# Attention with a gated feed-forward on one core: block 0's x in two loads, clock-keeping products up to K's arrival, V's first half by ScalarE's queue, K's second half copied by two engines side by side

## The chip, the cores and the metric

The kernel runs on one core of a Trainium2 chip. The metric is the device time of one execution in microseconds (us), lower is better. Every time comes from a real execution; every profile is one execution taken by the hardware profiler. Times inside a profile count from the start of its span.

## The reference, cut to what matters

```python
# x (1, 2048, 640), k_cache and v_cache (1, 32, 2048, 192), all bf16
xn = layernorm(x)
q  = (xn @ wq)                      # 32 heads of 192
p  = softmax(q @ k.T * 192 ** -0.5) # per head
s  = (p @ v) @ wo
g  = silu(ffn(xn))                  # silu(xn @ w1) * (xn @ w3) @ w2
return x + s * g
```

Keys and values are given, so nearly all the work is 32 heads of scores, exponentials and values. The change concerns only the first microseconds, in which nothing can run before the first x and K have arrived.

## The kernel before: the parts that matter

The 2048 queries are four blocks of 512, and a head's keys are eight pairs of 128. The opening works on head 0 and block 0. Loads are issued by SyncE (`nc.sync`), ScalarE (`nc.scalar`) and GpSimd (`nc.gpsimd`), each in program order.

```python
pk1 = ps_o.tile([P, 4, 512], BF16, tag="ob1", name="pk1")
warm = pk1[:, 0, 0:2 * P].bitcast(F32)

def turn_over(k):                    # products that only keep TensorE busy
    for i in range(k):
        nc.tensor.matmul(warm, lhsT=ident_bf[:], rhs=ident_bf[:], start=True, stop=True)

def head_start():
    for t in range(4):
        load_x(0, t, t + 1, nc.scalar if t % 2 else nc.sync)
    load_k0(0, nc.sync)              # head 0's K, first half
    turn_over(24)
    ln_stats(0, 0); ln_stats(0, 1); ln_stats_act(0, 3)
    load_w0(nc.scalar)               # head 0's weights
    load_k0(1, nc.scalar)            # K, second half
    load_x(1, queue=nc.scalar)       # block 1's x, 640 KB
    ...
    load_v(0, (0,), nc.gpsimd)       # head 0's V, first half
    load_w(1)                        # head 1's weights, GpSimd
    for i in range(4): ln_norm(0, i, nc.vector)
    turn_k0(pk0, 0, range(4))        # 16 transposes of K
    turn_over(12)
    ln_turn(0, 0, nc.scalar.copy)    # 10 transposes of x, one copy to xnT
    turn_over(4)
    ln_turn(0, 1, nc.vector.tensor_copy)
    swap_halves(0)                   # xnS: xnT with its partition halves swapped, by DMA
    copy_k0(nc.scalar.copy, pk0, 0, 0); copy_k0(nc.scalar.copy, pk0, 0, 1)
    load_v(0, (1,))                  # V, second half, SyncE
    load_x(2)                        # block 2's x, SyncE
    project_first()                  # block 0's queries
    turn_k0(pk1, 1, range(4))
    copy_k0(nc.scalar.copy, pk1, 1, 0)
    copy_k0(nc.vector.tensor_copy, pk1, 1, 1)
    scores(0); shift_first()
    shift_k0()                       # VectorE: a part of K to other partitions
    scores(1)
    ln_stats(1, 0); ln_stats(1, 1); ...   # block 1's layer norm, VectorE

# the stream that follows; n counts pairs
    if h == 0 and qb == 0 and p == 3:
        project(1, 0)                # head 1's queries: needs xnS and head 1's weights
    scores(n + 2)
    values(n)                        # needs V
    # p == 2: ln_stats(2, 0) on VectorE, needs block 2's x
    # p == 3: ln_turn(1, 1): transposes of block 1's second pair, needs a PSUM buffer
    #         that VectorE's cast of head 1's queries gives back
```

V's tile has rows of 194 elements, of which the load writes 192 (the next holds ones), so that each of its 1024 pieces per half is 384 B long:

```python
queue.dma_start(out=vt[:, t * NPAIR:(t + 1) * NPAIR, 0:DH],
                in_=A_v_cache[0, h, t * HK:(t + 1) * HK, :].rearrange("(i s) d -> i s d", i=P))
```

## Time and profile before

| what | before |
|---|---|
| time | 1943.08 us, median of 3 (1942.95 to 1943.15) |
| TensorE (PE) busy | 1930.2 of 1941.6 us |
| TensorE busy in 20 to 40 us | 18.77 of 20.00 |
| first values (needs V) | 17.48 us |
| block 2's x awaited until | 24.10 us |
| transposes of block 1's second pair | 25.84 us |

First the page of the kernel before: busy time of each engine.

```profile
span 1941.6 us, 59662 instructions
...
PE 1930.2 (99%) x27269; PEld 1318.6 (68%) x27277; DVE 654.5 (34%) x997; ACT 1181.1 (61%) x1278; POOL 281.0 (14%) x499
```

Then the busy time by stretches of the kernel before: microseconds busy in each stretch for each engine, the granted clock of TensorE (1.00 is full), the busy share of the DMA engines, and GB/s.

```profile
16.00:20.00 4.00, 3.46 (x50) 2.23 (x51) 3.80 (x13) 3.15 (x4) 0.57 (x1) 1.00 1.19 195
20.00:24.00 4.00, 3.79 (x47) 2.08 (x43) 2.98 (x10) 1.33 (x3) 0.83 (x2) 1.00 1.09 218
24.00:28.00 4.00, 3.15 (x52) 2.31 (x49) 3.04 (x7) 1.90 (x3) 1.61 (x3) 1.00 1.25 241
```

The DMA engines are busy throughout. TensorE is idle here and there, and from 60 to 1460 us never. The timeline of the kernel before shows why. Columns: start, length, engine, line, operation, what it writes and reads, shapes, count; in brackets how long the engine was idle before, and what ended that.

```profile
6.09 1.89 PE L271 MATMUL pk<-ident_bf,kn 128*128 128x128 bf16 x16 [1.98 <-DMA kn<-in_A_k_cache_dram]
...
8.96 0.72 PE L354 MATMUL pst<-ident_bf,xn 128*128 128x128 bf16 x10
...
10.99 2.34 PE L391 MATMUL ps<-xnT,W 128*128 128x256 bf16 x20 [0.53 <-ACT xnT L356]
...
14.27 1.01 ACT L277 COPY KW<-pk 128x1024 bf16<-128x1024 bf16 x1 [0.52 <-PE pk L271]
...
15.31 0.69 DVE L277 COPY KW<-pk 128x1024 bf16<-128x1024 bf16 x1 [1.19 <-ACT KW L277]
...
16.56 0.42 DVE L281 COPY KW<-KW 64x1024 bf16<-64x1024 bf16 x1
...
17.48 0.83 PE L516 MATMUL obank<-vt,pT 64*128 64x193 bf16 x16
...
24.10 0.89 DVE L316 BATCH_NORM_STATS2 stats<-x_all 128x6 f32<-128x320 bf16 x2 [0.22 <-DMA x_all<-in_A_x_dram]
...
25.15 0.64 DVE L429 CAST qA<-ps 128x512 bf16<-128x512 f32 x1
...
25.84 0.73 PE L354 MATMUL pst<-ident_bf,xn 128*128 128x128 bf16 x10 [0.85 <-DVE qA L429]
```

VectorE (DVE) copies its part of K's second half only after ScalarE (ACT) is done with the other. From 15.31 it has work up to the query cast at 25.15, for which TensorE waits. It stops for any length only twice on the way: 0.81 us for a result of GpSimd (ahead of 23.08), and 0.22 us for block 2's x, the only load in this stretch that it waits for.

V's first half was issued at 8.33 us and had landed at 14.8, 2.7 us before it was needed.

### The profile page before, as it was taken

How to read it: one execution, taken by the hardware profiler on the slowest of the kernel's cores; microseconds unless marked ns; L12 is line 12 of the kernel's file. 1: busy time of each engine (PE TensorE's matmuls, PEld its weight loads, DVE VectorE, ACT ScalarE, POOL GpSimd, SP SyncE). 2: the span in 40 equal slices, each digit the busy share in tenths (PEclk: the TensorE clock that was granted, in tenths of full speed). 3: DMA queues.
4: the chain of work that ended last, by engine and by line, in shares of the span. 5: the costliest groups of instructions: out<-in, count | busy, mean ns of one | idle time of the engine just before them, and what ended most of it. 6: DMA issues, size and time to landing. Idle time of an engine off the chain costs nothing.

```text
span 1941.6 us, 59662 instructions
## 1 busy us (share of the span) xinstructions
PE 1930.2 (99%) x27269; PEld 1318.6 (68%) x27277; DVE 654.5 (34%) x997; ACT 1181.1 (61%) x1278; POOL 281.0 (14%) x499
## 2 busy tenths in 40 slices
PE   8999999999999999999999999999999999999998
PEld 5666666666666666666666666666666666577776
DVE  7433333333333333333333333333333334521111
ACT  5667776767776767776777777677767677210000
POOL 2111111111111111111111111111111110000000
PEclk9999999999999999999999999999999999999999
DMA  8643433323233434363434343334334220937883
GB/s 174 135 98 67 98 71 71 88 58 91 59 93 68 94 64 101 68 161 68 100 66 101 68 100 68 98 67 100 69 61 94 62 74 2 252 74 136 154 151 62
DMA packets 395747, 178.98 MB, mean 92 GB/s; under 512 B 342480, under 2 KB 384176, under 8 KB 395488
## 3 DMA queue, kind: packets, MB, share of 16 engines
q1 hardware_dynamic: 371072, 124.99, 31.1%
q0 software_dynamic: 19424, 45.78, 9.9%
q8 instruction: 215, 3.52, 0.8%
q10 hardware_dynamic: 4992, 4.33, 0.7%
q14 instruction: 44, 0.36, 0.1%
HBM read 52.82 MB, written 27.79 MB: 42 GB/s over the span
## 4 chain that ended last, share of the span: by engine, by line
PE 98%; DMA 1%; DVE 0%; ACT 0%; SPq 0%; issue 0%; DVEq 0%; ACTq 0%
PE obank L516 35%; PE st L487 33%; PE ps L424 14%; PE ps_s L111 11%; PE ps_f L728 3%; PE ps_gu L702 1%; PE st L488 1%; DMA x_all<-in_A_x_dram 1%; PE ps L410 0%; DMA kn<-in_A_k_cache_dram 0%; PE pk L271 0%; DVE stats L316 0%; PE pst L354 0%; SPq L289 0%; ACT xnT L356 0%
## 5 line engine op out<-in xcount | busy, mean ns | idle before, releaser
L490 ACT ACTIVATE pT<-st 128x1024 bf16<-128x1024 f32 x1024 | 1047.2, 1023 | 252.3 <-PE st L488 237.0
L516 PEld LDWEIGHTS <-pT 64*128 64x128 bf16 x16384 | 713.7, 94 | 242.1 <-ACT pT L490 0.2
L516 PE MATMUL obank<-vt,pT 64*128 64x193 bf16 x16384 | 851.9, 243 | 0.0
L487 PE MATMUL st<-qC,KW 64*128 64x512 bf16 x2046 | 605.6, 376 | 0.4 <-DVE KW L281 0.3
L525 DVE COPY osum<-obank 128x772 f32<-128x772 f32 x128 | 123.1, 962 | 789.1 <-PE obank L516 789.1
L488 PE MATMUL st<-qB,KW 64*128 64x512 bf16 x1024 | 385.0, 376 | 0.0
L487 PE MATMUL st<-qA,KW 64*128 64x512 bf16 x1022 | 384.3, 376 | 0.5 <-ACT pT L490 0.4
L488 PE MATMUL st<-qC,KW 64*128 64x512 bf16 x1022 | 384.3, 376 | 0.0
L488 PE MATMUL st<-qA,KW 64*128 64x512 bf16 x1022 | 384.3, 376 | 0.0
L487 PEld LDWEIGHTS <-KW 64*128 64x128 bf16 x3068 | 277.9, 94 | 154.1 <-issue 2.1
L424 PE MATMUL ps<-xnT,W 64*128 64x512 bf16 x1280 | 297.2, 376 | 0.0
L424 PE MATMUL ps<-xnS,W 64*128 64x512 bf16 x1280 | 296.0, 376 | 0.2 <-DMA xnS<-xnT 0.2
L488 PEld LDWEIGHTS <-KW 64*128 64x128 bf16 x3068 | 278.0, 94 | 1.1 <-issue 0.7
L377 POOL DMA_DIRECT2D qC<-qA x124 | 65.8, 530 | 1284.4 <-DVE rl_all L532 1281.3
L430 ACT CAST qB<-ps 128x512 bf16<-128x512 f32 x131 | 76.8, 586 | 228.8 <-PE ps L424 223.3
L111 PE MATMUL ps_s<-wo_sb,oT 128*128 128x384 bf16 (+3 forms) x1535 | 208.8, 299 | 0.1
L424 PEld LDWEIGHTS <-W 64*128 64x128 bf16 x2560 | 122.8, 94 | 121.8 <-issue 0.6
L111 PEld LDWEIGHTS <-oT 128*128 128x128 bf16 x1536 | 148.4, 98 | 60.4
L526 DVE TENSOR_TENSOR osum<-osum,obank 128x772 f32<-128x772 f32 x128 | 122.7, 958 | 13.4
L533 DVE TENSOR_TENSOR ostage<-osum,rl_all 128x768 bf16<-128x768 f32 x128 | 122.6, 958 | 5.0 <-DMA o_scr<-ostage 0.7
L465 DVE SCALAR_TENSOR_TENSOR hT<-pt,qB 64x512 bf16<-64x512 bf16 x64 | 43.8, 684 | 198.6 <-ACT pt L464 198.6
L429 DVE CAST qA<-ps 128x512 bf16<-128x512 f32 x131 | 90.5, 691 | 25.1 <-PE ps L410 7.2
(82 smaller groups left out, 619.5 us busy)
## 6 DMA issues: line engine op xcount, KB each, us to landing
o_scr<-ostage SPq DMA_DIRECT2D x16, 1536.0 KB, 10.3
vt<-in_A_v_cache_dram SPq DMA_DIRECT2D x63, 384.0 KB, 5.6
qC<-qA POOLq DMA_DIRECT2D x248, 64.0 KB, 1.9
qC<-qB POOLq DMA_DIRECT2D x124, 64.0 KB, 2.1
wo_sb<-in_A_wo_dram POOLq DMA_DIRECT2D x1, 7680.0 KB, 36.8
W<-in_A_wq_dram POOLq DMA_DIRECT2D x31, 160.0 KB, 3.4
xnS<-xnT SPq DMA_DIRECT2D x8, 320.0 KB, 5.2
xt<-in_A_x_dram POOLq DMA_DIRECT2D x16, 160.0 KB, 9.0
```

What stands on the lines that cost most here:

```text
L111: nc.tensor.matmul(ps[:, 0:w], lhsT=oT[:, k, :], rhs=wo_sb[:, k, c0:c1], start=(k == 0), stop=(k == OC - 1))
L377: nc.gpsimd.dma_start(out=qC[0:64, half, :], in_=qAB[half][64:P, :])
L424: nc.tensor.matmul(ps[:, r * 512:(r + 1) * 512], lhsT=W[rows, j, :], rhs=xs[rows, j // 2, qs], start=(j == 0), stop=(j == 2 * DC - 1))
L429: a = nc.vector.tensor_copy(out=qAB[0][:], in_=ps[:, 0:512])
L430: b = nc.scalar.copy(out=qAB[1][:], in_=ps[:, 512:1024])
L487: nc.tensor.matmul(st2[:, 0:512], lhsT=ka, rhs=qa, start=r == 0 and nr == 3, stop=r == nr - 1)
L488: nc.tensor.matmul(st2[:, 512:1024], lhsT=kb, rhs=qb2, start=r == 0 and nr == 3, stop=r == nr - 1)
L490: nc.scalar.activation(out=pT2[:], in_=st2[:], func=ACT.Exp, scale=att_scale)
L516: nc.tensor.matmul(obanks[r][:, j * 256:j * 256 + DH + 1], lhsT=pT2[r * 64:(r + 1) * 64, t * 512 + j * P:t * 512 + (j + 1) * P], rhs=vt[r ...
L525: nc.vector.tensor_copy(out=osum[:], in_=ov[0])
L526: nc.vector.tensor_tensor(out=osum[:], in0=osum[:], in1=ov[1], op=ALU.add)
L533: nc.vector.tensor_tensor(out=ostage[:, qb * 4:qb * 4 + 4, hg * DH:(hg + 1) * DH], in0=osum[:, :, 0:DH], in1=rl.unsqueeze(2).to_broadcast( ...
```

## The change

The intent is to start the stream earlier. x of block 0 comes in two larger loads by one queue. More clock-keeping products run until K arrives, and fewer stand between K's transposes and those of x. V's first half leaves GpSimd, so that head 1's weights are issued sooner. VectorE and ScalarE copy their parts of K's second half at the same time. Much later, w2 comes in three pieces instead of two.

```diff
@@ copy_k0
-        copy(out=KW[:, 0:2, ks] if two == 0 else KW[:, 2:5:2, ks], in_=src[...])
+        return copy(out=KW[:, 0:2, ks] if two == 0 else KW[:, 2:5:2, ks], in_=src[...])
@@ loads_after
-            for c0, c1 in _pieces(FC, -(-FC // 2)):
+            for c0, c1 in _pieces(FC, -(-FC // 3)):
@@ head_start
-        for t in range(4):
-            load_x(0, t, t + 1, nc.scalar if t % 2 else nc.sync)
+        load_x(0, 0, 2)
+        load_x(0, 2, 4)
         load_k0(0, nc.sync)
-        turn_over(24)
+        turn_over(36)
 ...
         load_x(1, queue=nc.scalar)
+        load_v(0, (0,), nc.scalar)
 ...
-        load_v(0, (0,), nc.gpsimd)
 ...
-        turn_over(12)
+        turn_over(2)
 ...
-        copy_k0(nc.scalar.copy, pk1, 1, 0)
-        copy_k0(nc.vector.tensor_copy, pk1, 1, 1)
+        a = copy_k0(nc.scalar.copy, pk1, 1, 0)
+        b = copy_k0(nc.vector.tensor_copy, pk1, 1, 1)
+        tc.declare_no_dep(b.ins, a.ins, reason="two banks, two destinations")
```

More of the change, by code (lines that the diff above doesn't have):

```diff
@@ L276, in copy_k0 @@
         ks = slice(half * HP * P, (half + 1) * HP * P)
-        copy(out=KW[:, 0:2, ks] if two == 0 else KW[:, 2:5:2, ks], in_=src[:, 2 * two:2 * two + 2, :])
+        return copy(out=KW[:, 0:2, ks] if two == 0 else KW[:, 2:5:2, ks], in_=src[:, 2 * two:2 * two + 2, :])
     def shift_k0():
```

## The prediction

> **What bounds the kernel now.** TensorE: the page gives it 1930.2 us busy in a span of 1941.6 (99%). The busy table by stretches has it at 20.00 of 20.00 us in each stretch from 60 to 140, at 19.89 in 40 to 60, 18.77 in 20 to 40, 15.27 in 0 to 20. All of the change but w2's three loads (long before use) acts in the first 17 us: it can only remove TensorE idle time ahead of about 40 us, 0.3% at most.
>
> **Costs, from the opening's timeline.**
> - 36 instead of 24 warming products: 24 took 2.74 us from 1.38, then TensorE idled 1.98 us until K at 6.09. 36 end near 5.4, in idle time. The first 16 K transposes took 1.89 us, the second 16 (13.17) 1.06: the first met a slow clock. The Trainium skill (TensorE: Matmul & The Clock Gate, Part 1) has the clock double after some 3.4 us of sustained work in a free-running window; the trace agrees in kind (118 ns against 66 each). The first 16 may become partly fast.
> - 2 instead of 12 fillers: 12 took 1.34 us and ended at 9.1; the first two normalised tiles were ready at 8.2. The first x transposes and ScalarE's copy (9.71) come about 0.7 us earlier. The second pair is bound by VectorE (9.5): 0.1 to 0.2 only, so the half-swap copies of x (issued 11.40) gain about 0.2.
> - x in two loads on one queue: same bytes, same engines; arrival (VectorE began at 3.87, ScalarE at 4.72) within 0.3 us, if anything earlier. The skill (DMA: Bandwidth & Descriptors, "Issuing engines are not separate DMA queues") says several issuers save only issue time.
> - V's first half leaves GpSimd (1.06 us of issue); head 1's weights go out 1.1 us earlier. Neither is awaited.
> - K's second half side by side: VectorE's copy (0.69) waited 1.19 us for ScalarE's (1.01). VectorE is free about 0.9 us earlier; the shift of K that TensorE awaited at 17.03 ends near 16.0, and that wait (0.3 to 0.6 us) goes.
>
> Together TensorE reaches its steady stream (17.03 now) some 1.2 us earlier.
>
> **How much survives.** The chain of waits shows the next obstacle: x of block 2, issued at 14.32, landed 9.76 us later, at 24.08. VectorE's statistics wait for it, head 1's query cast stands behind them (25.15), and TensorE idles 0.85 us for that cast at 25.84. The DMA engines are busy throughout 10 to 24 us; the change moves no bytes away and fills the queues only some 0.3 us earlier. I expect this landing 0.2 to 1 us earlier, and most of the 1.2 us turned into longer waits at the half-swapped x (21.36) and before 25.84. Net gain about 0.6 us.
>
> **Prediction: 1942.4 us, 8 in 10 between 1941.2 and 1943.3.** Chances: faster by over 2% 0.005, within 2% 0.99, slower 0.005.
>
> **Right if the profile shows:** first x transposes near 8.3 instead of 8.96; VectorE's K copy beside ScalarE's; no wait on the K shift; block 2's x landing at 23.1 to 23.9; the wait ahead of 25.84 longer than 0.85 us. Wrong on the absorption if TensorE's idle in 20 to 40 has not grown from 1.23 us.
>
> **What would make it wrong.** Block 2's x landing over 1.5 us earlier, because queues interleave otherwise without V on GpSimd's (then up to 1.8 us gained); block 0's x landing clearly later on one queue; another phase of the slow clock.

## More of the kernel before

The DMA view of the kernel before over 6 to 20 us gives, for each queue, packets, MB and the time that its packets took; and for V's first half, from a narrower stretch, its size and the us from issue to landing. Queue q0 is GpSimd's (software), q10 ScalarE's, q1 SyncE's (hardware).

```profile
q1 hardware_dynamic: 1447, 0.98, 43.7%
q10 hardware_dynamic: 2256, 1.38, 33.7%
q0 software_dynamic: 272, 0.72, 21.5%
...
vt<-in_A_v_cache_dram POOLq DMA_DIRECT2D x1, 384.0 KB, 6.5
```

## The result, and the profile after

| | before | changed |
|---|---|---|
| median of 6 runs, us | 1943.21 (1942.95 to 1943.7) | 1943.32 (1943.2 to 1944.86) |
| ratio, 95% interval | | 1.0002 (0.999 to 1.0015) |
| first values, profiled run | 17.48 | 18.73 |
| block 2's x awaited until | 24.10 | 24.65 |
| transposes of block 1's second pair | 25.84 | 27.28 |

No difference is seen. The six times of the changed kernel are four between 1943.2 and 1943.35 and two at 1944.56 and 1944.86. The profiled run of the changed kernel is the slowest of its six, which has to be kept in mind.

The page of the changed kernel:

```profile
span 1943.0 us, 59675 instructions
...
PE 1931.9 (99%) x27279; PEld 1319.2 (68%) x27279; DVE 654.3 (34%) x997; ACT 1180.1 (61%) x1278; POOL 278.2 (14%) x498
```

The timeline of the changed kernel, the lines that answer to those shown of before:

```profile
5.95 1.07 PE L271 MATMUL pk<-ident_bf,kn 128*128 128x128 bf16 x16 [0.56 <-DMA kn<-in_A_k_cache_dram]
...
7.74 0.81 PE L354 MATMUL pst<-ident_bf,xn 128*128 128x128 bf16 x10 [0.61 <-DVE xn L346]
...
10.72 2.34 PE L391 MATMUL ps<-xnT,W 128*128 128x256 bf16 x20 [1.01 <-DVE xnT L356]
...
13.99 1.01 ACT L277 COPY KW<-pk 128x1024 bf16<-128x1024 bf16 x1 [0.52 <-PE pk L271]
13.99 0.69 DVE L277 COPY KW<-pk 128x1024 bf16<-128x1024 bf16 x1
...
15.24 0.42 DVE L281 COPY KW<-KW 64x1024 bf16<-64x1024 bf16 x1
...
18.73 1.04 PE L516 MATMUL obank<-vt,pT 64*128 64x193 bf16 x16 [1.92 <-DMA vt<-in_A_v_cache_dram]
...
24.65 0.89 DVE L316 BATCH_NORM_STATS2 stats<-x_all 128x6 f32<-128x320 bf16 x2 [2.08 <-DMA x_all<-in_A_x_dram]
...
26.07 0.69 DVE L429 CAST qA<-ps 128x512 bf16<-128x512 f32 x1 [0.29 <-PE ps L424]
...
27.28 0.73 PE L354 MATMUL pst<-ident_bf,xn 128*128 128x128 bf16 x10
```

Against this profile of before, the parts do what they were meant to up to 16 us: K's transposes take 1.07 us instead of 1.89, x's transposes start 1.22 us earlier, the two K copies start together, and VectorE's K shift starts 1.32 us earlier. (How long K's transposes take differs from one execution to the next: 1.73 and 1.59 us in the changed kernel's other two profiles, and 1.07 us in a second profile of before, shown in the fourth round, whose x transposes are as early without any change.) Part of it is lost at once: the first projection now waits 1.01 us for VectorE's copy and starts only 0.27 us earlier. Then two loads are late. TensorE, ready at 16.81, waits 1.92 us for V's first half, and VectorE waits 2.08 us instead of 0.22 for block 2's x.

The busy time by stretches of the changed kernel shows what follows: in 16 to 24 us the granted clock (third number from the end) is no longer 1.00.

```profile
16.00:20.00 4.00, 2.08 (x26) 1.33 (x27) 3.86 (x13) 1.87 (x2) 0.71 (x1) 0.90 1.15 182
20.00:24.00 4.00, 4.00 (x48) 2.98 (x46) 1.69 (x6) 1.72 (x2) 0.68 (x1) 0.67 1.26 259
24.00:28.00 4.00, 4.00 (x54) 2.51 (x52) 1.78 (x4) 1.94 (x3) 0.95 (x2) 1.00 0.72 223
```

TensorE ran at half clock for 3.4 us (the trace's clock record), which costs about half of that, an estimate of 1.7 us. The page agrees: TensorE is busy 1931.9 us, where two executions of the same kernel at full clock (below) have 1930.7 and 1930.5. "Busy 4.00 of 4.00" in 20 to 24 is therefore not progress.

The DMA view of the changed kernel, same stretches as before:

```profile
q10 hardware_dynamic: 3296, 1.77, 53.8%
q1 hardware_dynamic: 1012, 0.78, 35.4%
q0 software_dynamic: 160, 0.33, 12.6%
...
vt<-in_A_v_cache_dram ACTq DMA_DIRECT2D x1, 384.0 KB, 10.6
```

GpSimd's queue lost 272 - 160 = 112 packets and ScalarE's gained 3296 - 2256 = 1040. The same half of V, the same bytes, is about 100 packets when GpSimd issues it and about 1000 when ScalarE does. It now takes 10.6 us from issue to landing instead of 6.5.

**One point for all comparisons.** In every profile, 18 of 18, the time from the start of the transposes of block 1's second pair (25.84 in before) to the end of the span is between 1915.6 and 1916.0 us (before 1941.6 - 25.84 = 1915.8, changed 1943.0 - 27.28 = 1915.7). So all that differs between these executions happens ahead of this point, and w2's three pieces show no effect beyond 0.4 us. I call its start the common point.

### The profile page after: what moved, and what is told of

The parts are those of the page before. It is cut to its first block, busy times and chain, and to the rows that moved or that the text cites. A ratio compares the mean times of both kernels' runs of the same rounds, so it can differ in the third digit from the quotient of the medians. Undisturbed runs are those within 1.5% of the kernel's fastest.

```text
span 1943.0 us, 59675 instructions
## 1 busy us (share of the span) xinstructions
PE 1931.9 (99%) x27279; PEld 1319.2 (68%) x27279; DVE 654.3 (34%) x997; ACT 1180.1 (61%) x1278; POOL 278.2 (14%) x498
## 4 chain that ended last, share of the span: by engine, by line
PE 98%; DMA 1%; DVE 0%; ACT 0%; ACTq 0%; issue 0%; SPq 0%; DVEq 0%
PE obank L516 35%; PE st L487 33%; PE ps L424 14%; PE ps_s L111 11%; PE ps_f L729 3%; PE ps_gu L703 1%; DMA vt<-in_A_v_cache_dram 1%; PE st L488 1%; PE ps L410 0%; DMA x_all<-in_A_x_dram 0%; ACT pT L490 0%; DVE osum L526 0%; DVE osum L525 0%; ACT xn L338 0%; DVE stats L316 0%
## 5 line engine op out<-in xcount | busy, mean ns | idle before, releaser
L111 PE MATMUL ps_s<-wo_sb,oT 128*128 128x256 bf16 (+3 forms) x1536 | 208.8, 299 | 0.0
```

What stands on the lines that cost most here:

```text
L111: nc.tensor.matmul(ps[:, 0:w], lhsT=oT[:, k, :], rhs=wo_sb[:, k, c0:c1], start=(k == 0), stop=(k == OC - 1))
```

## The experiments

Sixteen runs were made, five timed rounds each, against before on the same chip. All gave correct results. Differences are of medians; the spread of one kernel is 0.5 to 4.6 us, so a few tenths mean nothing by themselves, and the profiles have to carry the argument. By the intervals (about 0.13% to either side, 2.6 us) every one of these kernels counts as the same as before; where a gain is claimed below, it rests on all five runs lying below all nine runs of before in the same job.

In the last column, "half-swapped x" is TensorE's wait for xnS, the copy of block 0's x with its halves swapped, and "cast" its wait for VectorE's query cast. A profile is of one execution, not of the median: it is the slowest of the five for x2_first and the fastest for changed_again, fill_v, fill_v_again, changed_third and rows_ahead_x2_first.

The expectations speak of theories. P: V's small pieces are to blame. Q: V's place at the end of its queue is. R: the change was worth nothing, since block 2's x sets the pace. D, later: whatever is gained is waited away at the next late load. G: two gates, VectorE's own chain and block 2's x, of which the later decides.

| run | median (range) | minus before | common point in its profile | what TensorE or VectorE waited for there |
|---|---|---|---|---|
| v_pool | 1943.74 (1942.91 to 1946.67) | +0.33 | 27.14 | half-swapped x 2.1, then half clock; block 2's x 2.74 |
| only_v | 1943.60 (1942.73 to 1944.44) | +0.19 | 26.02 | VectorE's chain |
| v_ahead | 1944.08 (1943.45 to 1945.42) | +0.67 | 27.09 | block 1's x 2.32, half-swapped x 1.1, block 2's x 0.42, cast 1.95 |
| v_whole_rows | 1942.73 (1942.64 to 1943.14) | -0.68 | 25.34 | V 1.25, block 2's x 1.79 |
| changed_again | 1943.61 (1942.80 to 1947.11) | -0.02 | 25.37 | half-swapped x 0.3, block 2's x 0.92 |
| fill_v | 1943.65 (1942.86 to 1944.95) | +0.02 | 25.43 | block 2's x 0.97 |
| x2_first | 1943.12 (1942.81 to 1944.12) | -0.51 | 26.40 | VectorE's chain |
| rows_ahead_x2_first | 1942.31 (1941.49 to 1942.94) | -1.32 | 24.05 | half-swapped x 0.4 |
| only_side | 1943.13 (1942.80 to 1944.45) | -0.43 | 25.38 | block 2's x 0.49 |
| side_x2_first | 1942.51 (1942.34 to 1942.91) | -1.05 | 25.04 | VectorE's chain |
| changed_x2_first | 1943.28 (1942.07 to 1946.65) | -0.28 | 25.09 | V 1.34 |
| pool_x2_first | 1942.37 (1942.03 to 1942.90) | -1.19 | 25.21 | half-swapped x 2.0, block 2's x 1.09 |
| changed_third | 1943.51 (1943.21 to 1946.14) | +0.18 | 25.79 | half-swapped x 0.86, block 2's x 1.46 |
| before_again | 1943.28 (1942.84 to 1943.54) | -0.05 | 25.60 | half-swapped x 0.94, block 2's x 1.04 |
| fill_v_again | 1943.73 (1943.19 to 1944.48) | +0.40 | 25.76 | block 2's x 1.46 |
| rows_ahead_x2_first_again | 1941.99 (1941.42 to 1943.02) | -1.34 | 24.54 | half-swapped x 1.4 |

### First round: is it V?

**v_pool**, the changed kernel with V's first half back on GpSimd:

```diff
         load_x(1, queue=nc.scalar)
-        load_v(0, (0,), nc.scalar)
 ...
+        load_v(0, (0,), nc.gpsimd)
         load_w(1)
```

> The changed kernel with only V's first half put back on GpSimd's queue, where it was before. Theory P (the hardware queue carries that half as 1024 pieces of 384 B, GpSimd's as some hundred of about 4 KB; the small pieces hold up V, the half-swapped x and block 2's x) and theory Q (V merely stands last in ScalarE's queue, behind the 640 KB of block 1's x) both say: TensorE's wait of 1.9 us for V is gone, V lands by 15 us, no execution shows a slow clock after 16 us, and the time is 0.4 to 1.3 us below before, about 1942.3. Theory R (the rest of the change was worth nothing to begin with, because block 2's x sets the pace) says 1943.2, within 0.2 of before.

Measured: 1943.74, no gain. The wait for V is gone, the first values start at 16.11, and the first projection at 10.00 without the wait of 1.01 us. But the half-swapped x is then late, and the half clock comes in spite of it (granted clock 0.89 in 20 to 24 us, 0.69 in 24 to 28). From v_pool's timeline:

```profile
10.00 2.55 PE L391 MATMUL ps<-xnT,W 128*128 128x256 bf16 x20
...
16.11 0.85 PE L516 MATMUL obank<-vt,pT 64*128 64x193 bf16 x16
...
21.89 0.39 PE L424 MATMUL ps<-xnS,W 64*128 64x512 bf16 x2 [2.10 <-DMA xnS<-xnT]
...
24.80 0.89 DVE L316 BATCH_NORM_STATS2 stats<-x_all 128x6 f32<-128x320 bf16 x2 [2.74 <-DMA x_all<-in_A_x_dram]
...
27.14 0.73 PE L354 MATMUL pst<-ident_bf,xn 128*128 128x128 bf16 x10
```

Theories P and Q, as the only cause, fall with this run: the gain is spent at another load. Theory R is nearer, although in this execution block 2's x was even later than in the changed one. The run also shows that the 1.01 us wait of the first projection comes with the moved V: all seven profiles of the changed kernel's opening with V loaded straight into its tile by ScalarE's queue have it, the two with V on GpSimd's queue do not. The queue by itself is not the cause: with V in whole rows on the same queue (v_whole_rows and both rows_ahead runs, below) the first projection starts at 9.95 to 9.98 without it. Why was not looked into.

**only_v**, the kernel before with only V's first half moved:

```diff
         load_x(1, queue=nc.scalar)
+        load_v(0, (0,), nc.scalar)
 ...
-        load_v(0, (0,), nc.gpsimd)
```

> The kernel before with only V's first half moved to ScalarE's queue. P and Q: V lands near 18.5 us, TensorE waits about 1 us for it at 17.5, and the time is 0.8 to 1.5 us above before, with some executions another 1.4 us longer where the clock drops after the wait. R: within 0.2 us of before.

Measured: 1943.60, no difference to be seen, against P and Q. V took 8.6 us from issue at 8.09, so it landed at 16.7, two us later than on GpSimd's queue; but TensorE, without the rest of the change, asks for it only at 17.96. The late V hurts only a kernel that is early.

**v_ahead**, the changed kernel with V ahead of block 1's x:

```diff
-        load_x(1, queue=nc.scalar)
         load_v(0, (0,), nc.scalar)
+        load_x(1, queue=nc.scalar)
```

> The changed kernel with V's first half issued ahead of block 1's x on ScalarE's queue. Q: V lands by 14.5 us, the wait is gone, and the time is as with V on GpSimd's queue, about 1942.3. P: V comes earlier, by 16.5 us, so its wait shrinks below 0.3 us, but the 1024 pieces are still in the way: the half-swapped x and block 2's x land no earlier than in the changed kernel less 0.5 us, and the time stays within 0.4 us of before.

Measured: 1944.08. V came in 5.8 us, at 13.5, in time for both P and Q; but block 1's x was then awaited 2.32 us and block 2's x until 25.35, as P had it for the later loads. Order in the queue moves the lateness from one load to the next; Q's gain is not there, and at 0.67 above before the time is also outside P's 0.4.

**v_whole_rows**, the same place in the queue, but into contiguous rows, and a copy by GpSimd from there into V's tile:

```diff
-        load_v(0, (0,), nc.scalar)
+        nc.scalar.dma_start(out=vs, in_=A_v_cache[0, 0, 0:HK, :].rearrange("(i s) d -> i (s d)", i=P))
 ...
         load_w(1)
+        nc.gpsimd.tensor_copy(out=vts[0][:, 0:NPAIR, 0:DH], in_=vs)   # vs: unused half of K's tile
```

> The changed kernel with V's first half loaded by the same queue at the same place into a buffer whose rows are contiguous (128 pieces of 3072 B), and copied from there into V's tile by GpSimd. P: the load lands by 15 us although it still stands last in ScalarE's queue; with GpSimd's copy of 2 to 3 us V is there by about 17.5, the wait for it is below 1 us, and block 2's x lands at least 1 us earlier than the 24.6 of the changed kernel; time 1942.2 to 1942.9. Q: the load lands near 18 us as before, the wait grows to over 3 us with the copy, and the time is above 1944.

Measured: 1942.73, with all five runs inside 0.5 us. The load landed in 7.5 us, at 15.7 (not by 15), GpSimd's copy took 1.46 us, and TensorE waited 1.25 us for it. Block 2's x was awaited until 23.60, 1.05 us earlier than in the first profile of the changed kernel, as P had said. Of 384 B pieces the same load at the same place took 8.5 to 10.6 us in the changed kernel's three profiles (8.6 to 10.3 in four more with other edits). With v_ahead (384 B pieces, ahead of block 1's x) and a later run (whole rows, ahead) the four cases stand side by side, in us from issue to landing:

| V's first half on ScalarE's queue | behind block 1's x | ahead of it |
|---|---|---|
| pieces of 384 B | 10.6, 8.6, 8.5 | 5.8 |
| whole rows of 3072 B | 7.5 | 4.6, 4.4 |

By these few profiles the place in the queue (theory Q) makes 3 to 5 us, the pieces (theory P) 1 to 3 us. Both are real for V itself; neither, alone, brings the whole gain back.

### Second round: loads or something else?

**changed_again**, the changed kernel itself:

> The changed kernel once more, for a second look at its spread and, with luck, a profile without the slow clock. Theory D (loads set the pace of the opening: whatever TensorE gains before 17 us it waits away at the next late load) says that the transposes of block 1's second pair, from which all profiles so far keep 1915.8 us to the end within 0.2, start at about 25.8 without the slow clock and near 27.2 with it, and that times fall in two groups, about 1943.2 and 1944.7.

Measured: 1942.80, 1943.09, 1943.61, 1943.67 and 1947.11. Its profile is of the fastest, without the half clock:

```profile
16.79 0.85 PE L516 MATMUL obank<-vt,pT 64*128 64x193 bf16 x16
...
23.63 0.89 DVE L316 BATCH_NORM_STATS2 stats<-x_all 128x6 f32<-128x320 bf16 x2 [0.92 <-DMA x_all<-in_A_x_dram]
...
25.37 0.73 PE L354 MATMUL pst<-ident_bf,xn 128*128 128x128 bf16 x10 [0.97 <-DVE qA L429]
```

In this execution V is in time (8.6 us after its issue at 8.19), block 2's x lands 1.02 us earlier than in the other profile, and 0.47 us of gain against the 25.84 of before is left. The same program thus differs by 2 us at V and by 1 us at block 2's x from one execution to the next. Theory D's 25.8 without the slow clock missed by 0.4 us, and 1947.11 belongs to neither of its two groups.

**fill_v**, and later **fill_v_again**, the changed kernel with clock-keeping products in the wait for V:

```diff
         scores(n + 2)
+        if n == 0:
+            turn_over(30)
         values(n)
```

> The changed kernel with 30 clock-keeping products (about 1.7 us at full clock) just ahead of the first values, in the time in which TensorE waits for V. If the slow clock comes from that wait, it is gone: no times near 1944.7, the five within 0.4 us around 1943.2, and a profile without half clock between 16 and 30 us. If the slow clock comes from something else, one or two of five lie near 1944.7.

> The changed kernel with 30 clock-keeping products ahead of the first values, a second time. If the slow clock after the wait for V makes the tail: none of five above 1944.2. If it makes only part of it: fewer and shorter than in the changed kernel's sixteen.

Measured: neither profile has a half clock in the opening, although V landed 9.7 and 10.3 us after issue. But the times reach 1944.38, 1944.48 and 1944.95, three of ten above 1944.2, against the five of sixteen above 1944.5, with up to 1947.11, of the changed kernel. The longest times are gone; the tail is not. The medians are no better, since 30 products also cost their time in executions in which V is early. Inconclusive as to how much of the tail is the clock.

**x2_first**, the kernel before with block 2's x ahead of V's second half:

```diff
-        load_v(0, (1,))
         load_x(2)
+        load_v(0, (1,))
```

> The kernel before with block 2's x issued ahead of V's second half on SyncE. Theory D: that x lands 1.5 to 3 us earlier than 24.1, the wait of 0.85 us before the transposes at 25.84 goes, they start near 25.0, and the time is 0.6 to 1.0 us below before. If the pace is set elsewhere (by VectorE's own work or by the half-swapped x), it is within 0.2 us of before.

Measured: 1943.12. Block 2's x is not awaited any more, yet TensorE still waits 1.1 us for the cast: VectorE arrives there 7.9 us after the end of its K shift (17.84 to 25.70) without any wait for a load. This profile is of the slowest of the five runs (1944.12), and the 0.51 us of the medians lies inside the spread, so it shows that a second gate exists, not that the load costs nothing. My expectation had read "VectorE waits for block 2's x" as the only gate, where the profile of before gives that wait 0.22 us. In before the two gates are nearly level: the load is the later by that 0.22 us, with VectorE's own chain just ahead of it.

**rows_ahead_x2_first**: V in whole rows ahead of block 1's x, and block 2's x ahead of V's second half, otherwise the changed kernel (the two edits above together). It ran again later as **rows_ahead_x2_first_again**.

> The changed kernel with V's first half in whole rows (128 pieces of 3072 B), ahead of block 1's x on ScalarE's queue and copied by GpSimd, and with block 2's x ahead of V's second half on SyncE. Theory D: V is there by 16.2 us, block 2's x lands by 22.5, only the half-swapped x is still awaited (1 to 2 us), the transposes start near 24.2, and the time is about 1941.6, below both kernels. If the wait for the half-swapped x trips the clock, some times are 1.5 us longer.

> The version with V's first half in whole rows ahead of block 1's x, and block 2's x ahead of V's second half, a second time on the chip of these runs: median 1.0 to 1.5 us below the kernel before, every run below the median of before, transposes of block 1's second pair at 23.9 to 24.6.

Measured: 1942.31 and 1941.99, 1.32 and 1.34 below before. All ten runs are below the lowest of the nine runs of before that each shared its rounds with (1942.97 and 1943.03), if the last by 0.01 only, and before_again, in the same job, went down to 1942.84. The common point is at 24.05 and 24.54. This is the fastest version, though the first median is 0.7 us above the 1941.6 that I had expected.

### Third round: two gates

**only_side**, the kernel before with K's second half copied side by side:

```diff
-        copy_k0(nc.scalar.copy, pk1, 1, 0)
-        copy_k0(nc.vector.tensor_copy, pk1, 1, 1)
+        a = copy_k0(nc.scalar.copy, pk1, 1, 0)
+        b = copy_k0(nc.vector.tensor_copy, pk1, 1, 1)
+        tc.declare_no_dep(b.ins, a.ins, reason="two banks, two destinations")
```

> The kernel before with only K's second half copied by the two engines side by side. Theory G (two gates stand before the transposes of block 1's second pair: VectorE's own chain, 7.8 us from the end of its K shift to the query cast, and the landing of block 2's x; the later one counts): VectorE's chain starts 0.8 to 1.0 us earlier, then waits about 1 us for block 2's x instead of 0.2; gain 0 to 0.5 us. If VectorE's chain were the only gate: gain 0.8 to 1.0.

**side_x2_first**, the same and block 2's x ahead of V's second half (the two diffs above).

> The kernel before with the side-by-side copies and block 2's x ahead of V's second half on SyncE. Theory G: neither gate is late, VectorE's chain runs without a wait for x, the transposes start about 1 us earlier than in before, and the time is 0.8 to 1.2 us below before, although block 2's x alone ahead gained at most some tenths. Against it: no more than 0.4 us.

Measured: 1943.13 for the first, with a spread that hides a few tenths, and 1942.51 for both together, 1.05 below before, all five runs below the lowest of nine before runs (1943.25). Each part alone leaves the other gate. From the timeline of side_x2_first:

```profile
16.07 0.42 DVE L281 COPY KW<-KW 64x1024 bf16<-64x1024 bf16 x1
...
24.34 0.64 DVE L429 CAST qA<-ps 128x512 bf16<-128x512 f32 x1
...
25.04 0.73 PE L354 MATMUL pst<-ident_bf,xn 128*128 128x128 bf16 x10 [0.62 <-DVE qA L429]
```

VectorE's chain now runs from the shift to the cast with no wait for x. This agrees with theory G: the later of VectorE's chain and block 2's x decides.

**changed_x2_first** and **pool_x2_first**: block 2's x ahead of V's second half in the changed kernel and in v_pool.

> The changed kernel with block 2's x ahead of V's second half, nothing else. Theory G: the wait for block 2's x is gone, so in executions in which V's first half is in time the transposes start near 24.2 and the time is about 1941.8; in the others TensorE waits up to 2 us for V, with or without the slow clock, and the time is 1942.5 to 1945. Median 1942.4, wide spread.

> The changed kernel with V's first half back on GpSimd's queue and block 2's x ahead of V's second half. Theory G: no wait for V, none for block 2's x, but one of 1 to 2 us for the half-swapped x, because the loads ahead of it are the same; transposes near 24.5, time about 1942.2; where that wait trips the clock, 1.5 us more.

Measured: 1943.28 (1942.07 to 1946.65) with V on ScalarE's queue, 1942.37 (1942.03 to 1942.90) with V on GpSimd's. The first missed the median of 1942.4 that I had expected by 0.9 us; in its profile TensorE waited 1.34 us for V and, up to the common point, for nothing after that. With the second the half-swapped x cost 2.0 us, without a half clock this time, and block 2's x was still awaited for 1.09 us, against what I expected. Between these two, V's queue is the only difference, and it is what separates a kernel with a tail from one without, once block 2's x is out of the way (five runs each, so this is likely rather than shown).

Put side by side, four runs with the rest of the change in place make a table of their own: V on ScalarE's queue and block 2's x where it was, -0.02 (changed_again); V back on GpSimd's, +0.33 (v_pool); block 2's x ahead, -0.28 (changed_x2_first); both, -1.19 us (pool_x2_first, all five runs below all nine of before). They ran in three jobs, each against its own before. Only with both loads out of the way does the gain appear.

### Fourth round: before and changed side by side

**changed_third** and **before_again**, both unedited:

> The changed kernel a third time. If a tail over a faster kernel is the cause: at least one of five near 1944.6 or above, the others between 1942.8 and 1943.4, and the profile's waits (V's first half, block 2's x) differ by more than 0.5 us from the two profiles so far. If block 2's x simply lands no earlier: all five within 0.4 us of the median of before.

> The kernel before as a run of its own, for a second profile. VectorE's chain is expected to run from the K shift to the query cast with a wait for block 2's x of 0.3 us at most, the transposes of block 1's second pair at 25.5 to 26.5 according to when the clock doubles, no half clock after that, times 1943.0 to 1944.1.

Measured: the changed kernel 1943.21, 1943.49, 1943.51, 1944.74 and 1946.14, so the tail is there again (two of the other three lie just above the 1943.4 that I had expected); before 1942.84 to 1943.54, without one. In the profile of before_again K's transposes took 1.07 us instead of 1.89, so that TensorE was as early as in the changed kernel, without any change of the code:

```profile
5.84 1.07 PE L271 MATMUL pk<-ident_bf,kn 128*128 128x128 bf16 x16 [1.73 <-DMA kn<-in_A_k_cache_dram]
...
7.81 0.81 PE L354 MATMUL pst<-ident_bf,xn 128*128 128x128 bf16 x10 [0.23 <-DVE xn L346]
...
9.93 2.34 PE L391 MATMUL ps<-xnT,W 128*128 128x256 bf16 x20
...
16.42 0.83 PE L516 MATMUL obank<-vt,pT 64*128 64x193 bf16 x16
...
21.03 0.39 PE L424 MATMUL ps<-xnS,W 64*128 64x512 bf16 x2 [0.94 <-DMA xnS<-xnT]
...
23.86 0.89 DVE L316 BATCH_NORM_STATS2 stats<-x_all 128x6 f32<-128x320 bf16 x2 [1.04 <-DMA x_all<-in_A_x_dram]
...
25.60 0.73 PE L354 MATMUL pst<-ident_bf,xn 128*128 128x128 bf16 x10 [0.94 <-DVE qA L429]
```

The first values start 1.06 us earlier than in the other profile of before, and the common point comes 0.24 us earlier. My expectation of at most 0.3 us of wait for block 2's x missed for that reason. That the clock was the cause is read from the durations only: the trace's clock record gives 1.00 around K's transposes in both profiles of before. Such an early start is the exception with before's opening: of the six profiles that have it (before, before_again, only_v, x2_first, only_side, side_x2_first) the other five have 1.89 us there and x's transposes at 8.7 to 9.0, while all twelve with the changed opening have them at 7.7 to 8.0. This is the absorption without any edit: an early TensorE and VectorE run into the same two loads. The changed kernel's third profile:

```profile
16.67 0.84 PE L516 MATMUL obank<-vt,pT 64*128 64x193 bf16 x16
...
21.21 0.39 PE L424 MATMUL ps<-xnS,W 64*128 64x512 bf16 x2 [0.86 <-DMA xnS<-xnT]
...
24.05 0.89 DVE L316 BATCH_NORM_STATS2 stats<-x_all 128x6 f32<-128x320 bf16 x2 [1.46 <-DMA x_all<-in_A_x_dram]
...
25.79 0.73 PE L354 MATMUL pst<-ident_bf,xn 128*128 128x128 bf16 x10 [0.95 <-DVE qA L429]
```

## Why the prediction was right or wrong

**Within 2%: right, and so is the frame.** Everything after the common point takes the same time within 0.4 us in all profiles.

**The upstream gains: right in part.** The copies start side by side (13.99 both), the wait on the K shift is gone, the scores of pair 2 go on without a gap. x's transposes came at 7.74 rather than 8.3, because TensorE starts with the first normalised tile and I had taken the ready time of both. The first projection gave most of this back in a wait of 1.01 us that I had not seen coming, and that comes with the moved V (see v_pool). Where V was in time, the first values started at 16.79 and 16.67, that is 0.7 to 0.8 us earlier than the 17.48 of before and not the 1.2 us of the prediction; against the 16.42 of before_again they are not earlier at all. VectorE's shift came 1.2 to 1.3 us earlier than in the first profile of before, a little more than predicted, and 0.1 to 0.3 us earlier than in before_again (15.50).

**The absorption: right in kind, wrong in size.** The prediction put it thus: "I expect this landing 0.2 to 1 us earlier". This is the term that failed. Block 2's x was awaited until 24.65, 23.63 and 24.05 us in three profiles of the changed kernel, against 24.10 and 23.86 in two of before: 24.1 against 24.0 in the mean, so no earlier. It was issued sooner, at 13.51, 13.59 and 13.05 us instead of 14.32 and 13.69, and took longer, 11.1, 10.0 and 11.0 us instead of 9.8 and 10.1. Without the slow clock, two changed executions have the common point at 25.37 and 25.79, before has it at 25.84 and 25.60: on these four, 0.1 us of gain in the mean, inside the difference between executions. In all four the common point follows 1.74 us after block 2's x is there, so the path that the prediction named (load, statistics, cast, TensorE) was right; the landing time put into it was not. The prediction's own test, that TensorE's idle time in 20 to 40 us must grow from 1.23 us, decides nothing: it was 1.45 and 1.99 in these two, but 2.05 in before_again (in the first profile of the changed kernel the half clock hides it).

I had also named only one gate of two. In the first profile of before, VectorE's own chain is only 0.22 us ahead of the load (x2_first removed the wait for block 2's x and gained nothing clear); the change makes VectorE early, and then the load alone decides. Three runs show the pair of gates: an early block 2's x and side copies gain nothing clear one at a time (x2_first, only_side), and 1.05 us together (side_x2_first).

**"Neither is awaited", of V's first half and head 1's weights: wrong for V.** It lands 8.5 to 10.6 us after issue instead of 6.5 and 5.7, so at 16.6 to 18.7 us instead of 14.0 to 14.8, and TensorE is early enough to wait for it, 1.92 us in one of the three profiles. I had counted GpSimd's issue time and forgotten to look at packets, although before's own DMA view has V's second half on a hardware queue with its many small packets. The Trainium skill (DMA: Bandwidth & Descriptors, "Issuing engines are not separate DMA queues") says that issuing from several engines saves only the issue time. I cited that for x, and took V's move to be as free. For x it held: VectorE began at 3.72, 3.85 and 3.75 us in the changed kernel's profiles, at 3.87 and 3.79 in those of before. V's move was not free: 1040 packets instead of 112, and a place behind 640 KB. The place weighs more for V itself: ahead of block 1's x the same small pieces landed in 5.8 us (v_ahead), as soon as through GpSimd's queue (5.7 to 7.2 us in seven profiles). The pieces then hold up what stands behind them: block 1's x took 9.7 us there, and 6.7 and 6.9 us behind whole rows. The same page ("Specifications") names 512 B as the least size for full rate; V's pieces are 384 B, and whole rows of 3072 B landed at least 1 us sooner at either place, which agrees in direction.

**The tail.** Over all jobs the changed kernel has five of sixteen runs at 1944.56 to 1947.11; 47 runs of before end at 1944.18. The other eleven changed runs lie between 1942.80 and 1943.67, where before lies too. In the one profiled member of the tail, what made it long is seen: a wait of 1.92 us for V, then 3.4 us of half clock. That all of them have this cause is not shown; the filling products took away the longest times but not all late ones, and v_pool has a tail with a wait for the half-swapped x instead.

**What stays open.** Why block 2's x lands no earlier although it is issued earlier is only partly settled: the DMA engines are busy throughout (a share above 1 in every stretch from 12 to 24 us), so that an earlier issue is an earlier place in the same crowd, but v_pool, with V in few packets, had that load latest of all but one. Executions of one program differ by 1 us there. Which load is served first was not controlled.

## What to carry to other kernels

In an opening filled by loads like this one, moving the compute earlier moved the waits and not the end: find each load that the earlier compute would meet, and its landing time, and move the loads together with the compute. Here two edits that gained little alone (side-by-side copies, and the awaited load ahead of one that is not urgent) gained 1.05 us together, and the whole change with V in whole rows and both V and the awaited load moved ahead 1.3 us. Before moving a load to another engine's queue, count its packets on both. When profiles of one program differ by a microsecond, take several before naming the gate.

## What the Trainium skill lacked or had wrong

- DMA: Bandwidth & Descriptors, "Issuing engines are not separate DMA queues": it says that issuing from several engines saves only issue time. What it lacks is that a move to another issuer can change a load's packets: here 384 KB into rows of 384 B with gaps were 112 packets issued by GpSimd and 1040 issued by ScalarE; by the few runs with whole rows, the small pieces make 1 to 3 us of the later landing. I found no page that gives the number of packets of pieces this small on the queues of ScalarE and SyncE.
- DMA: Bandwidth & Descriptors gives bandwidths and fixed costs, but not how far the landing of one load in a crowd varies: the same load of the same program landed at 23.63, 24.05 and 24.65 us.
- TensorE: Matmul & The Clock Gate, "Why this matters for your kernels", warns only of idle gaps above about 3 us. Here a wait of 1.92 us and one of 2.10 us (v_pool) were each followed by 3.4 us of half clock; waits of 1.34 us (changed_x2_first) and 1.98 us (pool_x2_first) were not. Its free-running window (Part 1) fits the opening: K's first transposes took 1.07 us in one execution of before and 1.89 us in another; the trace's clock record gives 1.00 for both, so the slow clock there is read from the durations.
